# Later attention units in half-height tiles of the matrix array, and a new written order

## The chip, the cores and the metric

The kernel runs on one core of one Trainium2 chip. The metric is the device time of one execution, in microseconds, as the median of several runs. Inside a core, TensorE multiplies matrices, VectorE (DVE), ScalarE (ACT) and GpSimd (POOL) do elementwise work, and SyncE (SP) issues DMAs. Each engine runs its own list of instructions in order and waits for the others through semaphores.

## The reference

Windowed attention over 4 batches, 8 heads, 576 positions and head size 64, followed by two gated feed-forward layers over the 2304 tokens. Heads 0 to 3 are "plain" (a window of 32 neighbours), heads 4 to 7 "dilated" (32 positions, every fourth one).

```python
scores = scale * np.matmul(q, k.transpose(0, 1, 3, 2))
mask_plain = (rel >= 0) & (rel < window)
mask_dil = (rel >= 0) & (rel < window * dilation) & (rel % dilation == 0)
scores = np.where(masks[None, :, :, :], scores, -1000000000.0)
attn = np.exp(scores - np.max(scores, axis=-1, keepdims=True))
attn = attn / (np.sum(attn, axis=-1, keepdims=True) + 1e-09)
x = np.matmul(attn, v)                      # tokens x 512
h = x @ w_in; x = (h - np.tanh(h)) @ w_out  # d_ff 2048
return ((x @ w1) * (x @ w2) @ w3) @ wo      # d_ff 1024
```

## The kernel before

The dilated heads are reordered on the host so that their window too is 32 neighbours. Attention is cut into 12 units: a batch times one third of the positions (three query tiles of 64). Each unit has two parts, `p` (plain heads) and `d` (dilated heads), and each part two pairs of heads; a pair's two heads lie one above the other in the 128 partitions of `q` and `k`. `q` is stored with zeros beside each head (lines 1149 to 1152, host code), so that a product over all 128 rows gives the scores of one head alone.

The scores of a part (`at_scores`, L480 to L512) begin with one bf16 product that writes the mask into PSUM (L496), and add 24 float32 products (L508): 32 queries by 64 keys each, on a tile of the array of 128 rows and 32 columns, four of which lie side by side. The compiler makes two TensorE instructions of each float32 product, so a unit has 96. The scores of the part's two pairs are interleaved in the free dimension (`k e`). VectorE takes the maximum and subtracts it (L526, L529), ScalarE the exponential (L535), VectorE sums and inverts (L541 to L546), GpSimd multiplies (L551). TensorE turns the result (`at_T`, L561, three transposes a part), ScalarE copies it out of PSUM twice, each time with a zero on every other row (`at_Tcopy`, L574), and TensorE multiplies it by `v` (`at_pv`, L592): 12 float32 products a part, 24 instructions, on tiles of 128 rows and 64 columns, two of which lie side by side, with 64 moving columns. ScalarE and VectorE split the result into two float32r summands in `X` (L614, L619).

The feed-forward layer runs in steps: `h` (L635, 12 float32r products of 128x128 weights), tanh, subtraction, split, `y` (L725, 12 products). The first feed-forward group (3 column blocks of d_ff) is woven into the attention by hand: the string `ORDER` lists words, and the program is written out in that order. A word is a letter, a number and, for parts, `p` or `d`: `q`, `v` load, `s` scores, `M` maximum, `E` exponential, `N` sum and inverse, `m` multiply, `T` transposes, `C` copies, `P` products with v, `X`, `L` the two summands; `w` loads a weight (512 KB), `a`, `b`, `c` rebuild its float32 value from float64 bits (ScalarE L144; VectorE L149 and L153; VectorE L159 and L162), `i`, `o` split it; `h`, `t`, `g`, `G`, `k`, `y`, `Y`, `Z` are the parts of a feed-forward step; `K` prepares masks. `q`, `v` and `w` all go through SP's one queue, in the order of the words. Units 0 to 2 have homes of their own for `q` and `v` (inside `Y` and `vhomes`), and their parts go one by one; from unit 3 on (`n >= PB`) scores, maximum, exponential and sum of both parts go together. Weights are staged in two buffers, so `w2` waits for `c0`, `w3` for `c1`. PSUM is tight: one tile of two banks for scores, one bank for transposes, two for `x`; two buffers `pb` (`NPB`) hold copied transposes.

The first dense product `h0` needs `L0p L1p L2p` (all positions of the plain heads) and `L0d L1d`. After the written order come the other feed-forward groups, then the second layer, which are dense products to the end.

Of the kernel before, what the change touches and what calls it, by code (L numbers as in the profile page):

```python
# [8 lines left out]
F32 = mybir.dt.float32  # L9
# [26 lines left out]
R = 4  # L36
# [17 lines left out]
i3 X2d M4 t1 a4 m3p T3p k0 o2 L2d q5p E4 q5d g1 o3 y0 w5 h2 v3p q6p G1 s5 C3p v3d b4 c4 t2 k1 m3d  # L54
T3d g2 q6d i4 o4 a5 N4 C3d h3 m4p M5 t3 E5 b5 P3p c5 v4p T4p v4d C4p y1 N5 X3p L3p g3 P3d G2 X3d m4d
T4d i5 k2 C4d L3d s6 M6 q7p q7d o5 P4p v5p X4p L4p h4 t4 m5p y2 Y2 G3 E6 P4d X4d w6 g4 h5 T5p Z2 C5p
m5d s7 N6 G4 L4d v5d P5p k3 y3 t5 g5 a6 X5p G5 T5d C5d w7 k4 a7 b6 k5 v6p m6p L5p y4 h6 M7 q8p t6
T6p c6 g6 q8d y5 q9p C6p i6 h7 G6 v6d E7 b7 t7 c7 g7 P5d N7 k6 w8 G7 Y5 m6d s8 q9d X5d P6p X6p Z5
T6d k7 h8 v7p m7p y6 L5d C6d P6d t8 M8 a8 E8 g8 G8 q10p m7d h9 N8 m8p X6d v7d T7p C7p s9 T7d o6 k8
t9 g9 y7 C7d h10 M9 t10 L6p g10 T8p G9 v8p E9 i7 N9 b8 P7p L6d X7p w9 y8 h11 k9 m8d L7p Y8 q10d s10  # L60
q11p G10 t11 C8p m9p P7d g11 q11d Z8 X7d P8p X8p L7d L8p T8d k10 y9 G11 M10 h12 c8 y10 E10 k11 C8d
t12 v8d m9d v9p a9 v9d y11 w10 T9p C9p g12 h13 G12 P8d b9 Y11 k12 Z11 t13 N10 m10p g13 T9d m10d G13
s11 M11 P9p X8d L8d C9d X9p k13 c9 E11 y12 w11 T10p h14 y13 C10p T10d t14 g14 a10 b10 G14 P9d k14
N11 m11p L9p C10d v10p h15 t15 v10d y14 g15 G15 Y14 h16 v11p T11p t16 k15 Z14 g16 y15 X9d o7 L9d G16
k16 m11d P10p X10p h17 C11p c10 t17 v11d P10d g17 G17 y16 L10p X10d T11d C11d h18 a11 t18 P11p X11p
L10d L11p P11d k17 X11d w12 g18 y17 L11d Y17 b11 Q0 i8 G18 i9 c11 h19 Z17 k18 t19 o8 g19 h20 G19 h21
w13 t20 y18 k19 i10 y19 h22 g20 t21 g21 G20 G21 k20 i11 k21 y20 a12 h23 b12 o9 a13 b13 t22 g22 G22
o10 o11 Z20 k22 Y20 h24 c12 t23 c13 g23 i12 y21 G23 y22 o12 k23 i13 y23 t24 g24 G24 o13 k24 Z23 Y23
"""


# [9 lines left out]
def attn_moe_kernel(  # L81
# [358 lines left out]
    def window(t, half):  # L440

        return 32 * half if t else 0

    def load_v(n, parts=AB):
        if n < NU:
            b, g = units[n]
            for ty in parts:
                v = v_home(n).rearrange("p (h t c) -> p h t c", h=2, t=TU)
                for e in range(2):

                    for t0, t1 in ((0, 1), (1, TU)) if g == 0 else ((0, TU),):
                        src = vt[b, 2 * ty + e, :HW, TU * g + t0:TU * g + t1].rearrange("k t c -> k (t c)")
                        ap = [list(d) for d in src.ap]
                        step = ap[0][0] * window(TU * g + t0, 1)
                        nc.sync.dma_start(
                            out=v[e:128:2, :, t0:t1].rearrange("k h t c -> k h (t c)"),
                            in_=bass.AP(tensor=src.tensor, offset=src.offset, ap=[ap[0], [step, 2], ap[1]]),
                        )
                vs[n, ty] = v

    NB = 2 * TU

# [4 lines left out]

    def bank_of(n, ty):

        if n >= PB:  # L470
            return ust[n]["both"][:, ty]
        m = order0.index((n, ty))
        if 2 <= m < 4:

            return yA.tile([128, 2, 256], F32, tag=f"y{m - 2}", name=f"s{m}").rearrange("p a c -> p (a c)")
        if m % 4 == 0:
            banks0["s"] = attn_pools["psS"].tile([128, 2, 512], F32, tag="s", name="s")
        return banks0["s"][:, m % 2]

    def at_scores(n, parts=AB):  # L480
        b, g = units[n]
        if n not in ust:
            ms = attn_pools["sm"].tile([128, 2, 2, NB], F32, tag="ms", name="ms")
            if n == 2:
                pm = Yf[:, KC * NT - 6 * KW - 2 * NB * HW:KC * NT - 6 * KW]
                pm = pm.rearrange("p (u i k e) -> p u i k e", u=2, i=TU, e=2)
            else:
                pm = attn_pools["pp"].tile([128, 2, TU, HW, 2], F32, tag="pm", name="pm")
# [3 lines left out]
        ps = ust[n]["ps"]  # L492
        for ty in parts:
# [20 lines left out]
    def of_parts(n, parts):  # L514

        s = ust[n]
        if len(parts) == 2:
            both = s["both"][:, :, :NB * HW].rearrange("p u (i k e) -> p u i k e", i=TU, e=2)
            return [(both, s["mx"], s["pm"], [128, 2, TU, HW, 2])]
        return [(s["ps"][u], s["mx"][:, u], s["pm"][:, u], [128, TU, HW, 2]) for u in parts]  # L520

    def at_max(n, parts=AB):
        for ps, mx, pm, shape in of_parts(n, parts):
            both = len(shape) == 5
            mx = mx.rearrange("p u (i e) -> p u i e" if both else "p (i e) -> p i e", e=2)
            nc.vector.tensor_reduce(  # L526
                out=mx, in_=ps.rearrange("p u i k e -> p u i e k" if both else "p i k e -> p i e k"), axis=AX.X, op=ALU.max
            )
            nc.vector.tensor_tensor(  # L529
                out=pm, in0=ps, in1=mx.unsqueeze(len(shape) - 2).to_broadcast(shape), op=ALU.subtract  # L530
            )

    def at_exp(n, parts=AB):
# [2 lines left out]

    def at_norm(n, parts=AB):
        s = ust[n]
        pm, sm = (s["pm"], s["sm"]) if len(parts) == 2 else (s["pm"][:, parts[0]], s["sm"][:, parts[0]])
        both = len(parts) == 2  # L540
        nc.vector.tensor_reduce(  # L541
            out=sm.rearrange("p u (i e) -> p (u i) e" if both else "p (i e) -> p i e", e=2),
            in_=pm.rearrange("p u i k e -> p (u i) e k" if both else "p i k e -> p i e k"), axis=AX.X, op=ALU.add
        )
        nc.vector.tensor_scalar(out=sm, in0=sm, scalar1=1e-9, scalar2=None, op0=ALU.add)
        nc.vector.reciprocal(out=sm, in_=sm)  # L546

    def at_mult(n, parts=AB):
        s = ust[n]
        for u in parts:  # L550
            nc.gpsimd.tensor_tensor(  # L551
                out=s["pm"][:, u], in0=s["pm"][:, u],
                in1=s["sm"][:, u].rearrange("p (i e) -> p i e", e=2).unsqueeze(2).to_broadcast([128, TU, HW, 2]),
                op=ALU.mult,
            )

    def at_T(n, parts=AB):
        for u in parts:
            pt = attn_pools["psT"].tile([128, TU, 128], F32, tag="t", name="t")
            for i in range(TU):  # L560
                nc.tensor.transpose(  # L561
                    pt[:, i], ust[n]["pm"][:, u, i].rearrange("p k e -> p (k e)"), id_sb
                )
            ust[n]["pt"][u] = pt

    npb = [0]
# [1 line left out]
    def at_Tcopy(n, parts=AB):  # L568
        for u in parts:
            pt = ust[n]["pt"][u]  # L570
            pb = ust[n]["pt"][u] = attn_pools["pb"][:, npb[0] % NPB]
            npb[0] += 1
            for e in range(2):
                nc.scalar.activation(  # L574
                    out=pb[:, :, :, e], in_=pt.rearrange("p i (j q) -> p i j q", j=4), func=ACTF.Copy,
                    scale=sel_sb[:, e:e + 1],
                )

    def at_pv(n, parts=AB):
        s = ust[n]  # L580
        for ty in parts:
            x = attn_pools["psX"].tile([128, 2, TU * QT], F32, tag="x", name="x")
            v = vs.pop((n, ty))
            for i in range(TU):
                for half, h in ((0, 0), (0, 1), (1, 0), (1, 1)):
                    dst = x[64 * h:64 * h + 64]
                    if ty:
                        dst = dst[:, :, QT * i + HQ * half:QT * i + HQ * half + HQ]
                    else:

                        dst = dst.rearrange("p e (r c l) -> p c e l r", r=R, l=HQ // R)[:, 2 * i + half]
                    nc.tensor.matmul(  # L592
                        out=dst, lhsT=v[:, half, i, D * h:D * h + D],
                        rhs=s["pt"][ty][:, i, 2 * h + half].rearrange("p a q -> p (a q)"), start=True, stop=True,
                    )
            s["x"][ty] = x

    def places(n, ty):

# [578 lines left out]
```

## Time and profile before

| | us |
|---|---|
| median of 3 runs | 800.28 (800.1 to 801.37) |
| the profiled execution, its own time | 802.01 |
| its span, first to last instruction | 800.2 |
| TensorE busy in it | 779.9 |
| VectorE busy | 548.1 |
| ScalarE busy | 292.8 |
| GpSimd busy | 158.3 |

The span leaves out 1.8 us of the profiled execution at its two ends. The page gives totals, forty slices, the DMA queues, the chain of work that ended last and the costliest lines; the timeline, the windows and the groups by line answer narrower questions.

### The profile page before, as it was taken

What the parts mean: (1) busy time and instruction counts of PE and PEld (TensorE: products, weight loads), DVE (VectorE), ACT (ScalarE), POOL (GpSimd) and SP (SyncE); (2) the same over time, 40 slices, a digit from 0 to 9 for tenths busy, and PEclk for the clock granted to TensorE, in tenths of its full rate; (3) what the DMA queues carried; (4) which work ended last, traced back from release to release, by engine and by line L of the source; (5) the groups of instructions that cost most, each with busy time, mean ns of one, the idle gap of its engine ahead of it and who ended that gap; (6) DMA issues with size and microseconds to landing.
All of it is one profiled execution on the core that took longest, in us unless ns stands there. A gap on an engine that the chain in (4) does not pass through costs nothing.

```text
span 800.2 us, 14174 instructions
## 1 busy us (share of the span) xinstructions
PE 779.9 (97%) x5592; PEld 688.0 (86%) x5592; DVE 548.1 (68%) x909; ACT 292.8 (37%) x546; POOL 158.3 (20%) x153
## 2 busy tenths in 40 slices
PE   5699999999999999999999999999999999999998
PEld 4589999888889888898888898799998999899996
DVE  4998675668888779987888889954454544734431
ACT  3566565443444444444444444321122111311111
POOL 3363343500022001210022223211121111211111
PEclk9799999999999999999999999999999999999999
DMA  9988742114455253632554344296203750156302
GB/s 300 302 247 294 236 155 73 53 53 126 150 160 158 105 162 116 186 119 66 156 155 136 105 134 131 93 340 211 93 1 115 238 187 1 41 181 202 118 1 79
DMA packets 62018, 115.58 MB, mean 144 GB/s; under 512 B 6400, under 2 KB 27008, under 8 KB 61952
## 3 DMA queue, kind: packets, MB, share of 16 engines
q1 hardware_dynamic: 61664, 114.32, 44.8%
q8 instruction: 44, 0.72, 0.4%
q10 hardware_dynamic: 288, 0.36, 0.2%
q14 instruction: 22, 0.18, 0.1%
HBM read 95.26 MB, written 19.40 MB: 143 GB/s over the span
## 4 chain that ended last, share of the span: by engine, by line
PE 89%; DVE 8%; ACT 1%; DMA 1%; issue 1%; ACTq 0%; SPq 0%; DVEq 0%
PE h L635 26%; PE y L725 25%; PE pr L979 22%; PE o L1042 6%; PE pr L1042 6%; PE x L592 2%; DVE a L159 2%; PE s L508 2%; DVE a L162 1%; DVE a L153 1%; PE t L561 1%; DVE a L149 1%; DVE Y L872 1%; DVE ms L541 1%; DMA id_sb<-in_ident 0%
## 5 line engine op out<-in xcount | busy, mean ns | idle before, releaser
L725 PE MATMUL y<-gs,LT 128*128 128x512 f32 (+1 forms) x520 | 121.9, 368 | 0.0
L725 PEld LDWEIGHTS y<-gs,LT 128*128 128x128 f32 x520 | 92.1, 188 | 16.3
L635 PE MATMUL h<-X,LT 128*128 128x512 f32 (+1 forms) x471 | 104.9, 370 | 0.0
L635 PEld LDWEIGHTS h<-X,LT 128*128 128x128 f32 x471 | 82.8, 188 | 15.2
L683 DVE TENSOR_TENSOR th<-h,th 128x512 f32<-128x512 f32 (+1 forms) x83 | 51.3, 618 | 58.5 <-ACT th L677 58.3
L979 PE MATMUL pr<-X 128*128 128x384 f32 x435 | 81.8, 334 | 0.0
L979 PE MATMUL pr<-X,LT 128*128 128x384 f32 x405 | 80.7, 336 | 0.0
L635 PE MATMUL h<-X,w 128*128 128x512 f32 (+1 forms) x381 | 78.8, 352 | 0.0
L677 ACT ACTIVATE th<-h 128x512 f32<-128x512 f32 (+1 forms) x83 | 44.8, 540 | 87.4 <-PE h L635 87.4
L979 PEld LDWEIGHTS pr<-X 128*128 128x128 f32 x435 | 76.2, 188 | 0.5
L159 DVE SCALAR_TENSOR_TENSOR a<-st,a 128x512 uint32<-128x512 uint32 x68 | 75.2, 1107 | 0.3
L979 PEld LDWEIGHTS pr<-X,LT 128*128 128x128 f32 x405 | 71.9, 188 | 1.3
L635 PEld LDWEIGHTS h<-X,w 128*128 128x128 f32 x381 | 62.8, 188 | 10.6 <-DVE th L683 0.2
L690 ACT ACTIVATE gs<-th 128x512 fp32r<-128x512 f32 (+1 forms) x83 | 47.9, 577 | 64.5 <-DVE th L683 57.5
L1016 DVE TENSOR_TENSOR u<-pr,u 128x384 f32<-128x384 f32 x72 | 40.1, 557 | 45.1 <-PE pr L979 38.5
L725 PE MATMUL y<-gs,w 128*128 128x256 f32 (+1 forms) x352 | 70.4, 330 | 0.0
L144 ACT ACTIVATE a<-st 128x512 f32<-128x512 f32 x68 | 45.5, 670 | 59.7 <-DMA st<-in_w 21.0
L992 ACT ACTIVATE cs<-u 128x384 fp32r<-128x384 f32 x24 | 12.6, 526 | 149.4 <-DVE u L1016 149.4
L1034 POOL TENSOR_TENSOR Y<-w,v 128x384 f32<-128x384 f32 x24 | 24.5, 1019 | 212.8 <-DVE w L1016 212.8
L725 PEld LDWEIGHTS y<-gs,w 128*128 128x128 f32 x352 | 54.6, 188 | 6.5
L162 DVE SCALAR_TENSOR_TENSOR a<-st,a 128x512 uint32<-128x512 uint32 x68 | 54.8, 806 | 2.3
L170 POOL TENSOR_TENSOR LT<-a,LT 128x512 fp32r<-128x512 f32 x18 | 25.8, 1436 | 152.2 <-ACT LT L167 152.2
(169 smaller groups left out, 1259.5 us busy)
## 6 DMA issues: line engine op xcount, KB each, us to landing
st<-in_w SPq DMA_DIRECT2D x28, 512.0 KB, 3.5
LT<-p SPq DMA_DIRECT2D x56, 256.0 KB, 4.2
X<-p SPq DMA_DIRECT2D x56, 256.0 KB, 4.7
st<-in_w_in SPq DMA_DIRECT2D x16, 512.0 KB, 4.2
st<-in_w_out SPq DMA_DIRECT2D x16, 512.0 KB, 4.1
q<-in_qz SPq DMA_DIRECT2D x18, 384.0 KB, 5.3
p<-LT SPq DMA_DIRECT2D x26, 256.0 KB, 4.5
v<-in_vt SPq DMA_DIRECT2D x32, 192.0 KB, 4.6
```

The costliest lines, as they stand in the source:

```text
L144: nc.scalar.activation(out=a.bitcast(F32), in_=st[:, :, 1].bitcast(F32), func=ACTF.Abs)
L159: nc.vector.scalar_tensor_tensor(out=a, in0=st[:, :, 1], scalar=0xC0000000, in1=a, op0=ALU.bitwise_and, op1=ALU.bitwise_or)
L162: nc.vector.scalar_tensor_tensor(out=a, in0=st[:, :, 0], scalar=29, in1=a, op0=ALU.logical_shift_right, op1=ALU.bitwise_or)
L170: nc.gpsimd.tensor_tensor(out=lo, in0=a.bitcast(F32), in1=hi.bitcast(F32), op=ALU.subtract)
L635: nc.tensor.matmul(out=ps, lhsT=a[sel[0]], rhs=b[sel[1]], start=(start and i == 0), stop=(i == n - 1), **kw)
L677: nc.scalar.activation(out=th[:, :tn], in_=gst[i][:, :tn], func=ACTF.Tanh)
L683: nc.vector.tensor_tensor(out=th[:, :tn], in0=ps[:, :tn], in1=th[:, :tn], op=ALU.subtract)
L690: nc.scalar.activation(out=gs[:, 0, :tn], in_=th[:, :tn], func=ACTF.Copy)
L725: nc.tensor.matmul(out=y[k], lhsT=wt[sel[0]][:, 128 * k:128 * k + 128], rhs=gs[:, sel[1], tn * m:tn * m + tn], start=(cs[m] == 0 and n == ...
L979: nc.tensor.matmul(out=ps[:, :TP], lhsT=s[e][:, 128 * k:128 * k + 128], rhs=(hi, lo)[f][1][k], start=start and n == 0, stop=n == 5, skip_g ...
L1016: nc.vector.tensor_tensor(out=out, in0=ps[:, :TP], in1=x, op=op)
L1042: nc.tensor.matmul(out=tiles[m], lhsT=cs[e][:, 128 * m:128 * m + 128], rhs=WW[j][f], start=begin and n == 0, stop=end and n == 2,)
```

## The change

The change concerns units 3 to 11 and the written order; the arithmetic is the same.

Scores (`scores_by_rows`): each product now takes only the 64 rows of its own head, on a tile of 64 rows and 32 columns. The two heads of a pair lie on the two row halves and write to the two banks of the unit's PSUM tile; the two pairs of heads lie on different columns. There are as many products as before, 48 a unit, 96 instructions, now on eight tiles. Two mask products a unit, as before.

Everything after the scores is laid out with the 64 keys of one head next to each other, plain and dilated side by side, so that a transpose puts the plain keys of a head on one row half and the dilated on the other. One copy a part then suffices, without zeros. The products with v (`at_pv`) take 64 rows, 64 columns and 32 moving columns, on four tiles: 48 products a unit, 96 instructions, where there were 24 and 48. They now come once a unit, `P3` instead of `P3p` and `P3d`, and need both transposes' copies (both `pb` buffers) and both `x` banks at once. `v` is loaded so that one buffer holds one pair of each kind, each kind on 64 neighbouring partitions, in the same number of DMAs and bytes.

For units 0 to 2 only the PSUM banks of the scores change: every third score tile takes a bank of the `s` tile, the others `y0` and `y1`.

The words are the same but for `P`; they stand in a new order throughout. Up to `h0`:

```diff
-K0 K1 q0p q1p s0p q2p q0d M0p q1d s1p E0p s2p s0d M1p N0p m0p w0 T0p E1p C0p N1p M2p q2d M0d E2p m1p
-N2p T1p v0p s1d v1p m2p s2d w1 a0 E0d C1p T2p b0 P0p C2p N0d c0 M1d X0p M2d E1d v2p a1 m0d L0p b1
-T0d q3p E2d P1p C0d w2 a2 q3d P2p N1d c1 m1d T1d s3 N2d C1d i0 m2d i1 T2d b2 c2 v0d v1d X1p L1p w3
-P0d o0 X2p L2p o1 X0d i2 M3 P1d L0d X1d E3 a3 L1d q4p q4d h0 v2d s4 N3 C2d P2d w4 b3 t0 g0 h1 G0 c3
...
+w0 q0p q1p w1 q2p q0d a0 b0 K0 K1 c0 s0p s1p s2p q1d q2d a1 w2 M0p v0p E0p M1p i0 b1 c1 s0d M2p N0p
+E1p E2p m0p i1 M0d v1p s1d E0d N1p m1p a2 T0p M1d C0p N2p E1d m2p s2d q3p q3d v2p T1p P0p C1p T2p
+C2p N0d M2d X0p w3 m0d b2 P1p N1d q4p m1d s3 o0 o1 X1p c2 L0p L1p T0d C0d v0d a3 T1d P2p E2d X2p P0d
+q4d v1d M3 E3 s4 v2d b3 c3 i2 L2p C1d N2d N3 X0d m2d w4 P1d L0d X1d q5p m3p T2d C2d L1d a4 h0 M4 t0
+g0 P2d q5d T3p b4 E4 o2 w5 i3 N4 G0 m3d h1 s5 C3p o3 t1 k0 T3d g1 v3p v3d h2 m4p a5 X2d C3d q6p q6d
...
```

After `h0` the products with v stand in 17 separate blocks on TensorE before (a neighbouring pair of parts twice) and in 10 after; `s4` stands behind `h0` before and ahead of it after. The rest of the diff, cut to its core:

```diff
     def bank_of(n, ty):
-        if n >= PB:
-            return ust[n]["both"][:, ty]
         m = order0.index((n, ty))
-        if 2 <= m < 4:
...
-        if m % 4 == 0:
+        if m % 3:
+            y = yA.tile([128, 2, 256], F32, tag=f"y{m % 3 - 1}", name=f"s{m}")
...
+    def scores_by_rows(n, g):
...
+        for i in range(TU):
+            t = TU * g + i
+            for ty in AB:
+                k, q = kq[ty]
+                for h in range(2):
+                    r = slice(64 * h, 64 * h + 64)
+                    for e in range(2):
+                        for half in range(2):
+                            k0 = KS[t] - KS[TU * g] + window(t, half)
+                            j, c = 2 * e + half, QT * h + HQ * half
+                            nc.tensor.matmul(
+                                out=ps[HQ * j:HQ * j + HQ, h, i, 1 - ty], lhsT=q[r, e, i, c:c + HQ],
+                                rhs=k[r, e, k0:k0 + HW], start=False, stop=(i == TU - 1 and ty == 1),
+                                skip_group_check=True, tile_position=(64 * h, HQ * j),
+                            )
...
     def at_Tcopy(n, parts=AB):
...
+            if n >= PB:
+                pb = ust[n]["pt"][u] = pb.rearrange("p i j e q -> p (i j e q)")[:, :TU * 128]
+                nc.scalar.activation(out=pb, in_=pt.rearrange("p i c -> p (i c)"), func=ACTF.Copy)
+                continue
             for e in range(2):
                 nc.scalar.activation(
...
     def at_pv(n, parts=AB):
...
+        for i in range(TU):
+            for half in range(2):
+                for e in range(2 if n >= PB else 0):
+                    for ty in AB:
+                        r = slice(HW * (1 - ty), HW * (1 - ty) + HW)
+                        for h in range(2):
+                            c = 128 * i + QT * e + HQ * half
+                            nc.tensor.matmul(
+                                out=x_part(n, ty, i, half, h)[:, e], lhsT=v[e][r, half, i, D * h:D * h + D],
+                                rhs=s["pt"][h][r, c:c + HQ], start=True, stop=True,
+                                tile_position=(r.start, 64 * h),
+                            )
...
```

## Rows read from the trace of the kernel before

**Rows 1.** Page, parts 1 and 2: engine totals; GB/s over 40 slices of 20 us

```profile
PE 779.9 (97%) x5592; PEld 688.0 (86%) x5592; DVE 548.1 (68%) x909; ACT 292.8 (37%) x546; POOL 158.3 (20%) x153
...
GB/s 300 302 247 294 236 155 73 53 53 126 150 160 158 105 162 116 186 119 66 156 155 136 105 134 131 93 340 211 93 1 115 238 187 1 41 181 202 118 1 79
```

**Rows 2.** Windows: length, busy us of PE, PEld, DVE, ACT, POOL, clock, DMA share, GB/s

```profile
0.00:36.85 36.85, 21.29 (x530) 16.60 (x530) 26.26 (x52) 15.11 (x30) 12.23 (x24) 0.89 0.93 297
36.85:130.00 93.15, 92.74 (x1731) 86.02 (x1730) 69.33 (x124) 58.34 (x128) 38.25 (x42) 0.99 0.70 222
...
32.00:36.00 4.00, 1.90 (x36) 1.90 (x38) 3.90 (x5) 0.31 (x1) 1.03 (x1) 0.50 1.00 320
```

**Rows 3.** Timeline, TensorE to 40 us: start, length, count, idle before and releaser

```profile
5.75 0.48 PE L496 MATMUL s<-mask_sb,id_sb 128*128 128x384 bf16 x1 [5.75 <-DVE mask_sb L375]
...
34.10 2.83 PE L592 MATMUL x<-pb,v 128*64 128x64 f32 x48 [2.55 <-DVE X L619]
...
36.85 2.83 PE L635 MATMUL h<-X,WG 128*128 128x256 f32 x12
```

**Rows 4.** Timeline, TensorE: one unit's mask and scores at full clock

```profile
64.27 0.49 PE L496 MATMUL s<-mask_sb,id_sb 128*128 128x384 bf16 x2
64.69 1.55 PE L508 MATMUL s<-k,q 128*32 128x64 f32 x96
66.16 0.92 PE L592 MATMUL x<-pb,v 128*64 128x64 f32 x24
```

**Rows 5.** Timeline, TensorE: blocks with v between dense blocks

```profile
121.35 0.92 PE L592 MATMUL x<-pb,v 128*64 128x64 f32 x24
122.20 1.68 PE L635 MATMUL h<-X,w 128*128 128x256 f32 x12
123.81 0.92 PE L592 MATMUL x<-pb,v 128*64 128x64 f32 x24
...
128.02 1.62 PE L592 MATMUL x<-pb,v 128*64 128x64 f32 x48
129.57 1.68 PE L725 MATMUL y<-gs,w 128*128 128x256 f32 x12
131.09 1.59 PE L635 MATMUL h<-X,WG 128*128 128x256 f32 x12
132.52 1.52 PE L635 MATMUL h<-X,w 128*128 128x256 f32 x12
```

**Rows 6.** Lines L508, L592: weight loads of 32 and 64 columns, min/median/max ns

```profile
L508 PEld LDWEIGHTS s<-k,q x864: 106/110/177, 28.4 to 108.2; 128*32 128x32 f32 x173
...
L592 PEld LDWEIGHTS x<-pb,v x576: 132/138/227, 19.7 to 129.4; 128*64 128x64 f32 x192
```

**Rows 7.** DMA issues: KB each, median us to landing

```profile
st<-in_w_in SPq DMA_DIRECT2D x16, 512.0 KB, 4.2
...
q<-in_qz SPq DMA_DIRECT2D x18, 384.0 KB, 5.3
...
v<-in_vt SPq DMA_DIRECT2D x32, 192.0 KB, 4.6
...
k<-in_kT SPq DMA_DIRECT2D x12, 224.0 KB, 5.0
```

**Rows 8.** Lines by shape, VectorE, first 38.1 us (last row whole span)

```profile
L162 DVE SCALAR_TENSOR_TENSOR a<-st,a 128x512 uint32<-128x512 uint32 x3 | 4.0, 1345 | 0.1
L526 DVE TENSOR_REDUCE ms<-s 128x6 f32<-128x384 f32 x6 | 3.3, 546 | 4.3 <-PE s L508 4.3
L159 DVE SCALAR_TENSOR_TENSOR a<-st,a 128x512 uint32<-128x512 uint32 x3 | 2.9, 983 | 0.0
...
L153 DVE TENSOR_SCALAR a<-a 128x512 uint32<-128x512 uint32 x3 | 2.3, 766 | 0.1
...
L149 DVE TENSOR_SCALAR a<-a 128x512 f32<-128x512 f32 x3 | 1.2, 396 | 0.0
...
L541 DVE TENSOR_REDUCE ms<-pm 128x12 f32<-128x768 f32 x9 | 8.5, 950 | 1.9 <-ACT pm L535 1.9
```

More of the change, by code (lines that the diff above doesn't have):

```diff
@@ L55 @@
[L55 to L59, printed above, removed]
@@ L444, in load_v @@
     def load_v(n, parts=AB):
[L445 to L459, printed above, removed]
+        if n >= NU:
+            return
+        b, g = units[n]
+        for part in parts:
+            v = v_home(n).rearrange("p (h t c) -> p h t c", h=2, t=TU)
+            for other in range(2):
+                if n < PB:
+                    rows, ty, e = slice(other, 128, 2), part, other
+                else:
+                    rows, ty, e = slice(HW * other, HW * other + HW), 1 - other, part
+                for t0, t1 in ((0, 1), (1, TU)) if g == 0 else ((0, TU),):
+                    src = vt[b, 2 * ty + e, :HW, TU * g + t0:TU * g + t1].rearrange("k t c -> k (t c)")
+                    ap = [list(d) for d in src.ap]
+                    step = ap[0][0] * window(TU * g + t0, 1)
+                    nc.sync.dma_start(
+                        out=v[rows, :, t0:t1].rearrange("k h t c -> k h (t c)"),
+                        in_=bass.AP(tensor=src.tensor, offset=src.offset, ap=[ap[0], [step, 2], ap[1]]),
+                    )
+            vs[n, part] = v
     NB = 2 * TU
@@ L492, in at_scores @@
         ps = ust[n]["ps"]
+        if n >= PB:
+            scores_by_rows(n, g)
+            return
         for ty in parts:
@@ L512, in at_scores @@
                         )
-    def of_parts(n, parts):
-        s = ust[n]
[L517 to L527, printed above, removed]
-            )
+    def scores_by_rows(n, g):
+        ps = ust[n]["both"][:, :, :NB * HW].rearrange("p h (i u k) -> p h i u k", i=TU, u=2)
+        m0 = mask_sb[:, M_DIL[g]:M_DIL[g] + TU]
+        ap = [list(d) for d in m0.ap]
+        ap.insert(2, [ap[1][0] * (M_PLAIN[g] - M_DIL[g]), 2])
+        for h in range(2):
+            nc.tensor.matmul(
+                out=ps[:, h], lhsT=id16_sb, rhs=bass.AP(tensor=m0.tensor, offset=m0.offset, ap=ap),
+                start=True, stop=False, skip_group_check=True,
+            )
+        kq = [ks.pop((n, ty)) for ty in AB]
+        for i in range(TU):
[12 more added lines that the diff above has]
+                                skip_group_check=True, tile_position=(64 * h, HQ * j),
+                            )
@@ new lines, in at_max @@
+    def at_max(n, parts=AB):
+        s = ust[n]
+        if n >= PB:
+            ps = s["both"][:, :, :NB * HW].rearrange("p h (b k) -> p h b k", k=HW)
+            pm = s["pm"].rearrange("p h (b k) -> p h b k", k=HW)
+            nc.vector.tensor_reduce(out=s["mx"], in_=ps, axis=AX.X, op=ALU.max)
+            nc.vector.tensor_tensor(
+                out=pm, in0=ps, in1=s["mx"].unsqueeze(3).to_broadcast([128, 2, NB, HW]), op=ALU.subtract
+            )
+            return
+        for u in parts:
+            ps, pm = s["ps"][u], s["pm"][:, u].rearrange("p (i k e) -> p i k e", i=TU, e=2)
+            mx = s["mx"][:, u].rearrange("p (i e) -> p i e", e=2)
+            nc.vector.tensor_reduce(out=mx, in_=ps.rearrange("p i k e -> p i e k"), axis=AX.X, op=ALU.max)
@@ L529, in at_max @@
             nc.vector.tensor_tensor(
-                out=pm, in0=ps, in1=mx.unsqueeze(len(shape) - 2).to_broadcast(shape), op=ALU.subtract
+                out=pm, in0=ps, in1=mx.unsqueeze(2).to_broadcast([128, TU, HW, 2]), op=ALU.subtract
             )
@@ L538, in at_norm @@
         s = ust[n]
[L539 to L546, printed above, removed]
+        for sm, pm in ([(s["sm"], s["pm"])] if n >= PB else [(s["sm"][:, u], s["pm"][:, u]) for u in parts]):
+            if n >= PB:
+                out, src = sm, pm.rearrange("p h (b k) -> p h b k", k=HW)
+            else:
+                out = sm.rearrange("p (i e) -> p i e", e=2)
+                src = pm.rearrange("p (i k e) -> p i e k", i=TU, e=2)
+            nc.vector.tensor_reduce(out=out, in_=src, axis=AX.X, op=ALU.add)
+            nc.vector.tensor_scalar(out=sm, in0=sm, scalar1=1e-9, scalar2=None, op0=ALU.add)
+            nc.vector.reciprocal(out=sm, in_=sm)
     def at_mult(n, parts=AB):
@@ L581, in at_pv @@
         for ty in parts:
[L582 to L591, printed above, removed]
+            s["x"][ty] = attn_pools["psX"].tile([128, 2, TU * QT], F32, tag="x", name="x")
+        v = {part: vs.pop((n, part)) for part in parts}
+        for i in range(TU):
[3 more added lines that the diff above has]
+                        r = slice(HW * (1 - ty), HW * (1 - ty) + HW)
+                        for h in range(2):
+                            c = 128 * i + QT * e + HQ * half
+                            nc.tensor.matmul(
+                                out=x_part(n, ty, i, half, h)[:, e], lhsT=v[e][r, half, i, D * h:D * h + D],
+                                rhs=s["pt"][h][r, c:c + HQ], start=True, stop=True,
+                                tile_position=(r.start, 64 * h),
+                            )
+                for h in range(2 if n < PB else 0):
+                    ty = parts[0]
                     nc.tensor.matmul(
-                        out=dst, lhsT=v[:, half, i, D * h:D * h + D],
+                        out=x_part(n, ty, i, half, h), lhsT=v[ty][:, half, i, D * h:D * h + D],
                         rhs=s["pt"][ty][:, i, 2 * h + half].rearrange("p a q -> p (a q)"), start=True, stop=True,
                     )
-            s["x"][ty] = x
     def places(n, ty):
```

56 lines of the change are left out of this document (34 added, 22 removed).

## The prediction

> **What bounds the kernel.** I read the page's totals first, then windows by stage, then TensorE's timeline. TensorE is busy 779.9 of 800.2 us [rows 1]. The windows split that: up to 36.85 us, where the first dense product `h0` begins, it is busy 21.29 us and idle 15.56; from there to 130 us, the end of attention, it is busy 92.74 of 93.15 [rows 2]. Beyond 130 us only dense products follow, which the change leaves alone. So from `h0` on, time is TensorE's work, and a microsecond taken off TensorE there is a microsecond off the end, as long as the others keep up: VectorE is busy 69.33 of these 93.15 us, ScalarE 58.34, the DMAs 0.70 [rows 2]. Ahead of `h0` TensorE isn't the limit. It waits for VectorE at 5.75 us and again at 34.10 [rows 3], VectorE is busy 26.26 of 36.85 us, and the DMAs are busy 0.93 of the time at 297 GB/s [rows 2]; the slices show hardly more than that anywhere in attention (300, 302, 247, 294) [rows 1]. The end is therefore: the time at which `h0` starts, plus TensorE's work from there (800.20 - 36.85 = 763.35 us now), plus new idle time.
>
> **Scores.** A unit's 96 score instructions take 1.47 us of TensorE, from 64.69 to the next block at 66.16 [rows 4], 15.3 ns each on four tiles side by side. An instruction with v has the same 64 moving columns, with two tiles side by side: 24 more of them in one block cost 1.55 - 0.85 = 0.70 us [rows 5], 29 ns each. So twice as many tiles halve the price, and per tile both come to about 60 ns. [...] Eight tiles then give about 7.5 ns each. What doesn't shrink is the change of tile shape at both ends of a block: a block of 24 with v takes 0.85 us, of which 0.70 is its 24 instructions, so 0.15 is fixed [rows 5]. A unit saves (1.47 - 0.15) / 2 = 0.66 us. No row shows row halves; the bounds are 0 (they take turns) and 0.66, and I take 0.66, because the columns do run side by side. The two heads write to different banks, so the banks give no reason against. Seven units (5 to 11) stand behind `h0` in both orders: -4.6 us. `s3` stands ahead of it in both. `s4` moves ahead of it, and its slot with its masks, here as in unit 6 64.27 to 66.16, goes: -1.9 us.
>
> **Products with v.** There are 96 instructions a unit for 48, on four tiles for two: per tile as many as now. Each has half the moving columns but loads the same 64 weight columns. Loads of 32 columns show 110 ns, of 64 columns 138 [rows 6], which is 0.88 ns a column, so 64 columns are about 56 ns (an estimate from this difference), as long as today's whole interval of 58 ns per tile; 32 moving columns would be half of that. The load sets the pace, and I take no change of the stream, 1.40 us a unit. The bounds: the interval halves with the moving columns (-0.70 a unit, -6.3 for nine units), or the row halves take turns (+1.40, +12.6). What does go is blocks: 17 behind `h0` become 10. One block in place of two saves 2 x 0.85 - 1.55 = 0.15 us inside, and a dense block between two of them takes 1.61 us where one away from them takes 1.43 [rows 5], so about 0.2 more; I take 0.35 x 7 = -2.5 us, with bounds of 1.0 and 3.1.
>
> [...]
>
> **Start.** The queue of loads decides first. `P1d`, the last product ahead of `h0`, needs `v1d`. Ahead of it and with it the new order sends four weights (512 KB each), ten parts of `q` (384 KB and about 215 KB of `k` each; five units, where four units' parts stood before), five parts of `v` (two DMAs of 192 KB each) and the masks [rows 7]: about 10.4 MB, where the old order sends 8.7. At 297 GB/s, start included, that is 35 us against 29. Then come `P1d` (1.4 us at half clock, from the 2.75 us for two parts), its copy, and `h0`: 37.5 us at the earliest. VectorE is the second limit. `b3`, `c3` and `N3` now stand ahead of `L1d`: 0.4 + 0.8 + 1.0 + 1.3 us and about 1.5 us (0.95 of it the sum) [rows 8], 5 us more. Part of them finds room: `b0` and `c0` go to the front, into the 5.75 us in which all waited for masks and the 4.3 us in which VectorE waited for scores [rows 3, 8]. But `b0` stands ahead of `K0` on VectorE and needs `w0`, which shares the first microseconds with the masks, so the first mask product comes at some 8 us in place of 5.75; what hides that is the loads, which couldn't feed scores faster anyway. In sum `L1d` moves from about 38 to 39.5 us. I put `h0` at 39.0 (37.5 to 42), +2.15 us. `h0` begins at a low clock now, 0.50 in the stretch ahead of it, after idle time on TensorE [rows 2], and its 12 products take 2.83 us where they take some 1.6 later [rows 3, 5]; the new order idles there as well, and I count it as equal.
>
> **Behind h0.** The new layout gives ScalarE one copy a part for two, about 10 us less in all, on an engine that isn't the limit; VectorE and GpSimd do the same operations on neighbouring instead of interleaved elements, counted at nothing since neither is full. The new waits: `P` of a unit needs both copies and both `x` banks, so it waits for the last `L` of the unit before, and `h`, `y`, `T` behind it in TensorE's queue wait too; the next unit's first copy waits for `P` to free a `pb` buffer, and tanh and the splits queue behind that copy on ScalarE. Between two `P` some four dense blocks (6 us) lie, enough for chains of 2 to 3 us. Loads are closer: `q5`, needed by `s5` three blocks behind `h0`, ends at about 12 MB, 41 to 44 us, just when `s5` is due. New idle time: +1.0 us (0 to 4).
>
> **Sum.** Work from `h0` on: 763.35 - 4.6 - 1.9 - 2.5 = 754.35. With `h0` at 39.0 and 1.0 idle, the span is 794.35, 5.85 less. Against the profiled execution (802.01, span 800.2 and 1.8 around it) that is 796.2; the median of the runs shown is 800.28, 1.7 below it, so the forecast is 794.4.
>
> **Rivals.** (1) Row halves take turns on TensorE. Scores save nothing (+4.6 behind `h0`), and products with v cost double, 1.40 x 9 = +12.6: 811.6 us. It decides the sign once more than about a third of that price comes true (5.9 of 17.2). For it speaks that no tile of fewer than 128 rows is in this trace; against it that tiles divided by columns do run together. (2) Issue is the floor: 15.3 ns is what an instruction costs at least. Scores save nothing (+4.6), v costs 96 x 15.3 = 1.47 for 1.40 (+0.6): 799.6, no change. [...] (3) Weight loads of 64 rows aren't the pace, and v halves: 794.4 - 6.3 = 788.1. [...] (4) The start or the loads limit: `h0` at 42 and 4 us of idle time give 800.4.
>
> **Chances.** Forecast 0.64 (790 to 798.5), v halves 0.10, loads limit 0.10, issue floor 0.07, turns 0.09. A difference under 0.2%, 1.6 us, can't be told from none here: same is 798.7 to 801.9. Faster: 0.64 + 0.10 + 0.01 of the floor + 0.03 of the loads = 0.78; same 0.10; slower 0.12. The range 787 to 801 holds the forecast, v halved, the floor and most of the loads' case, and leaves out the turns.
>
> **What would show it.** A unit's scores should take 0.81 us from start to the next block, its products with v 1.5 us in one block of 96; `h0` should begin near 39 us with `s4` behind it already, and TensorE should show under 2 us of idle time to the end of attention, which should come near 124 us. Scores at 1.47 with v at 1.5 would be the floor; v near 3 us the turns; v near 0.85 the third rival; idle time ahead of `s5` or the early `P` the loads. I would be wrong most easily in the start, which rests on a count of bytes.

## The result, and the profile after

The changed kernel takes 807.45 us (median of 4 runs, 807.13 to 809.77), the kernel before 800.39 beside it: a ratio of 1.0092, 95% interval [1.0072, 1.0113]. It is slower, by 7 us or 0.9%, where 794.4 was forecast, and the range (787 to 801) doesn't hold it. The profiled execution took 807.13 us, of which 805.30 are the span.

The page first (parts 1 and 3): TensorE runs 432 more product instructions than before, and as many more weight loads, and is busy 3.4 us less [rows 1]; the queue `q8` of kind "instruction" carries 47 packets.

```profile
span 805.3 us, 15000 instructions
...
PE 776.5 (96%) x6024; PEld 684.9 (85%) x6024; DVE 541.6 (67%) x909; ACT 282.5 (35%) x528; POOL 156.3 (19%) x153
...
q8 instruction: 47, 0.77, 0.4%
```

Windows by stage (length, busy us of PE, PEld, DVE, ACT, POOL, clock, DMA share, GB/s): to `h0`, from there to the first dense product of 512 columns, which is the end of attention's work, and the rest.

```profile
0.00:39.89 39.89, 22.07 (x628) 16.65 (x629) 26.20 (x59) 17.20 (x33) 15.39 (x27) 0.89 0.96 306
39.89:138.94 99.05, 92.38 (x2098) 86.65 (x2097) 64.15 (x117) 47.36 (x113) 36.27 (x41) 0.98 0.69 192
138.94:805.30 666.36, 662.07 (x3302) 581.55 (x3300) 451.29 (x734) 217.93 (x384) 104.60 (x85) 1.00 0.40 127
```

Before, the same two marks stand at 36.85 and 133.88 us ([rows 2] ends the stretch at 130 us):

```profile
36.85:133.88 97.03, 96.62 (x1764) 89.90 (x1763) 73.11 (x131) 60.92 (x134) 39.99 (x44) 0.99 0.67 213
133.88:800.20 666.32, 662.01 (x3302) 581.53 (x3300) 448.78 (x728) 216.75 (x382) 106.07 (x86) 1.00 0.40 126
```

The rest hasn't moved. `h0` came at 39.9, near the forecast (39.0). The loss is in the middle: with 4.6, 1.9 and 2.5 us off and 1.0 of new idle time it should have been 89.0, and it is 99.05, of which TensorE is idle 6.67 (0.41 before). This is what those idle times wait for:

```profile
PE x L638 <- issue: 4.2, 3, 2.4
PE s L542 <- DMA q<-in_qz: 1.3, 1, 1.3
PE h L687 <- issue: 0.7, 1, 0.7
PE x L638 <- DMA v<-in_vt: 0.5, 2, 0.3
```

"issue" means that the profile shows no semaphore that held the instruction back: 4.9 of the 6.67 us have no releaser. Such an idle time is called a pause here. The timeline of TensorE (start, length, count, idle before) shows the blocks at their good and at their bad:

```profile
67.02 1.17 PE L542 MATMUL s<-k,q 64*32 64x64 f32 x96
68.12 1.70 PE L777 MATMUL y<-gs,WG 128*128 128x256 f32 x12
69.75 1.36 PE L638 MATMUL x<-pb,v 64*64 64x32 f32 x78
71.40 0.53 PE L638 MATMUL x<-pb,v 64*64 64x32 f32 x18 [0.29 <-issue]
...
78.63 1.59 PE L638 MATMUL x<-pb,v 64*64 64x32 f32 x95
82.57 0.21 PE L638 MATMUL x<-pb,v 64*64 64x32 f32 x1 [2.35 <-issue]
82.71 0.90 PE L598 MATMUL t<-id_sb,pm 128*128 128x128 f32 x3
83.27 2.62 PE L777 MATMUL y<-gs,w 128*128 128x256 f32 x12
85.73 1.57 PE L687 MATMUL h<-X,w 128*128 128x256 f32 x12
...
93.42 1.60 PE L638 MATMUL x<-pb,v 64*64 64x32 f32 x96
94.95 0.55 PE L598 MATMUL t<-id_sb,pm 128*128 128x128 f32 x3
```

A unit's scores take 1.10 us here to the next block, and 1.17 on average over the seven units behind `h0`, waits left out (forecast 0.81, 1.47 before [rows 4]); its products with v take 1.53 (93.42 to 94.95; forecast 1.5). At 78.63 one block stops after 95 of its 96 products for 2.35 us, with nothing to wait for. Behind this pause TensorE also runs at a lower clock: the `y` block at 83.27 takes 2.46 us to the next one, where 1.45 is usual, in a window whose granted clock is 0.55. The shorter pauses at 60.57 and 70.89 us have no such window behind them: from 60 to 78 us the granted clock is 1.00.

```profile
78.63:82.57 3.94, 1.59 (x96) 1.49 (x96) 0.98 (x2) 1.23 (x2) 0.00 (x0) 0.93 0.94 322
82.57:85.73 3.16, 3.16 (x16) 3.02 (x16) 0.00 (x0) 1.28 (x4) 0.00 (x0) 0.55 1.10 252
```

**Where the pauses sit.** I counted TensorE's list (products, weight loads and its own semaphore instructions, in order) and looked up the pauses, and the packets of `q8` beside them. One of 0.34 us at 23.20 us (place 662) is left out, since run 3 puts the same wait down to GpSimd (`POOL pm`):

```
place in list   mod 256   TensorE stands (start to start)   q8 packet        end to restart
  449             193       16.25 to 17.70                   15.02 - 16.11    1.59
 1217             193       35.97 to 37.50                   35.24 - 36.20    1.30
 2241             193       60.57 to 62.30                   59.69 - 60.74    1.56
 2753             193       70.89 to 71.40                   68.52 - 69.86    1.54
 3265             193       80.00 to 82.57                   80.11 - 81.03    1.54
 4801             193      114.81 to 115.81                 112.93 - 114.27   1.54
```

All six stand at the same place of a block of 256, and TensorE goes on 1.3 to 1.6 us after a packet of 16 KB has landed. 47 packets, at 256 entries each, would be 12,032, and the list has some 12,180 entries. Before it had 11,330, by 44 packets, and no idle time of 0.05 us or more at such a place. The page of before has:

```profile
q8 instruction: 44, 0.72, 0.4%
```

So the reading to be tested: the list reaches TensorE in blocks of 256, each by one packet, and these blocks come too late. A unit has 96 entries more than before. (The expectations below count 542 and 446 a unit; from the masks of `s3` to the dense part, over nine units, it is some 533 now and 439 with the old products in the same order.) The packet of 80.11 us shared the DMA engines with loads that kept them busy; this is the DMA view from 78.63 to 82.57 us:

```profile
DMA packets 977, 1.27 MB, mean 322 GB/s; under 512 B 59, under 2 KB 896, under 8 KB 976
...
q1 hardware_dynamic: 976, 1.25, 92.7%
q8 instruction: 1, 0.02, 1.5%
...
v<-in_vt SPq DMA_DIRECT2D x4, 192.0 KB, 8.8
```

### The profile page after: what moved, and what is told of

Its sections match the earlier page's. It is cut to its first block, busy times and chain, and to the rows that moved or that the text cites. A ratio compares the mean times of both kernels' runs of the same rounds, so it can differ in the third digit from the quotient of the medians.

```text
span 805.3 us, 15000 instructions
## 1 busy us (share of the span) xinstructions
PE 776.5 (96%) x6024; PEld 684.9 (85%) x6024; DVE 541.6 (67%) x909; ACT 282.5 (35%) x528; POOL 156.3 (19%) x153
## 4 chain that ended last, share of the span: by engine, by line
PE 88%; DMA 4%; DVE 4%; SPq 2%; issue 1%; ACT 1%; ACTq 0%
PE h L687 26%; PE y L777 24%; PE pr L1031 22%; PE o L1094 6%; PE pr L1094 6%; DMA v<-in_vt 2%; PE x L638 2%; PE s L542 1%; DMA st<-in_w_out 1%; DVE a L159 1%; DMA st<-in_w_in 1%; PE t L598 1%; DVE a L162 1%; SPq L460 1%; DVE Y L924 1%
## 5 line engine op out<-in xcount | busy, mean ns | idle before, releaser
L159 DVE SCALAR_TENSOR_TENSOR a<-st,a 128x512 uint32<-128x512 uint32 x68 | 73.7, 1083 | 0.4
L162 DVE SCALAR_TENSOR_TENSOR a<-st,a 128x512 uint32<-128x512 uint32 x68 | 51.6, 759 | 2.3
```

Of the source, the lines that this page charges most:

```text
L159: nc.vector.scalar_tensor_tensor(out=a, in0=st[:, :, 1], scalar=0xC0000000, in1=a, op0=ALU.bitwise_and, op1=ALU.bitwise_or)
L162: nc.vector.scalar_tensor_tensor(out=a, in0=st[:, :, 0], scalar=29, in1=a, op0=ALU.logical_shift_right, op1=ALU.bitwise_or)
```

## The experiments

The expectations set a theory of late instructions against rivals: first, that the new order costs the time; later, that the length of the list costs it whatever the data do. "Stretch" is `h0` to the first 512-column product, "dense part" what follows it.

**1 and 2: the two halves of the change alone.** The first has the old tiles and products in the new order and the joined blocks; the second the new tiles in the old order, the joined block where the later of the two stood.

```
e1: -P3            e2: -P3p ... P3d       (units 3 to 11)
    +P3p P3d           +        P3
```

> Old products (128 rows) and old layout, written in the new order (each P as both parts in turn). Theory A, late instructions: TensorE's gaps without a releaser in the changed kernel (7.3 us to 120 us, each at an instruction whose place in TensorE's list is 193 more than a multiple of 256) come from a denser instruction stream; with 446 instead of 542 instructions a unit they go, scores cost 0.33 us a unit more (9 units, +3): about 802 us. Theory B, the order itself is the loss: the gaps and the late start stay and the scores cost more: 809 to 811 us.

Measured: 798.68 us against 800.56, ratio 0.9981 [0.9970, 0.9992]. The stretch:

```profile
37.30:129.67 92.37, 92.20 (x1667) 86.60 (x1666) 64.42 (x117) 57.95 (x131) 36.47 (x42) 1.00 0.67 210
```

Idle 0.16 us, and 97.03 - 92.37 = 4.66 us less than before; the prediction's terms for `s4` and the blocks were 1.9 + 2.5 = 4.4. The order costs nothing. It is a small gain, 1.9 us by the medians and 4.1 by the spans of the two traces (796.1 for 800.2): the stretches here and below are those of one execution each, and run 1's ten executions lie between 797.5 and 800.7 us. Theory A had the time 3 us too high, but the pauses at place 193 are gone as it said, except one of 1.59 us at place 1217, ahead of `h0`. So what makes the change slow comes with the new tiles and their layout.

> New products and layout, written in the old order; only the products with v of a unit are joined (put where the last of their inputs is ready, the plain part's X and L behind them, h12 and t12 behind L8p), and four half-size buffers for copied transposes stand in the place of two. Theory A: the gaps without a releaser stay (5 to 8 us), against 3 us won by scores and 3 by joined blocks: 801 to 804 us. Theory B: the old order gives 794 to 796 us, as the prediction's sum has it without the start.

Measured: 828.07 us, ratio 1.0343. Neither theory gave this: in the old order a joined block waits for the splits of the unit before and for its own `v`, which two blocks a stage apart did not. The waits of TensorE from 35 to 161 us:

```profile
PE x L640 <- DVE X L673: 6.0, 2, 4.2
PE x L640 <- DMA v<-in_vt: 5.9, 2, 3.7
PE x L640 <- issue: 2.3, 2, 1.5
```

The run says that the new order is needed for joined blocks, and nothing of the instructions.

**3: the same kernel, its list moved by 128 entries.** 64 products of 64 columns on the zero tile are put ahead of everything.

```
-ORDER = "w0 q0p ..."
+ORDER = "S64 w0 q0p ..."
```

> The changed kernel with 64 small products (128 instructions) that nothing uses at the head of TensorE's list, where it waits for masks. Theory A: the gaps stay at places that are 193 more than a multiple of 256 and so fall on other products, 128 instructions earlier in the program; their sum changes (4 to 9 us) and the time with it, 803 to 810 us. Theory C, the products or their tiles themselves stall: the gaps stay at the same products and the time within 1 us of 807.5.

Measured: 807.53 us, ratio 1.0089. That the time is that of the changed kernel is chance: in the trace `h0` comes at 36.13 us, the stretch takes 101.61 with 10.13 idle, and the dense part 1.7 us more. The pauses: places 705, 961, 1217, 1473, 1985, 2241, 2753, 3265 and 4289, every one 193 above a multiple of 256. The instructions that stand at these places are now others: from `h0` on, two `h` blocks (3.0 us idle) and a block with v of an early unit, in old tiles (2.0 us), which had no pause there, and three blocks with v in new tiles (3.8 us). Two of these three paused in the changed kernel too, after 78 and after 95 of their 96 products. Here it is after 14 and after 31, earlier by just the 64 products that were put ahead:

```profile
68.71 0.43 PE L638 MATMUL x<-pb,v 64*64 64x32 f32 x14
70.25 1.47 PE L638 MATMUL x<-pb,v 64*64 64x32 f32 x82 [1.11 <-issue]
...
78.37 0.66 PE L638 MATMUL x<-pb,v 64*64 64x32 f32 x31
80.56 1.14 PE L638 MATMUL x<-pb,v 64*64 64x32 f32 x65 [1.53 <-issue]
```

So it is the place in the list and not what the instruction does.

**4: less data.** From the fourth unit on the 64-row tiles read only half of each `q` tile; the other half are zeros which the old tiles needed. Loading without them saves 3.5 MB and leaves the list as it is.

```
-q = home(n, 2 * TU * 2 * QT, ...); out=q, in_=qz[...]
+q = home(n, 2 * TU * QT, ...);     out=q, in_=qc[...]      # n >= PB
```

> The changed kernel, but from unit 3 on q is loaded without its zeros, which 64-row products don't need: 192 KB in place of 384 for each of 18 parts, 3.5 MB less in all. Theory A, with transfers of instructions waiting behind transfers of data: gaps without a releaser shrink by 2 to 4 us, the waits for q (1.7 us) go: 802 to 805 us. If the gaps had nothing to do with transfers: only the waits for q go, 805 to 806.5 us.

Measured: 799.55 us, ratio 0.9987 [0.9977, 0.9997]: 8 us come back with the same list, more than either theory gave. `h0` 36.87, and the stretch:

```profile
36.87:130.26 93.39, 90.70 (x2099) 84.75 (x2098) 64.06 (x117) 47.58 (x113) 37.04 (x42) 1.00 0.65 178
...
PE s L544 <- issue: 1.2, 1, 1.2
PE x L640 <- issue: 1.0, 3, 0.5
PE h L689 <- issue: 0.3, 1, 0.3
```

Idle is 2.69 for 6.67 us, and the granted clock of the stretch is 1.00 (0.98 in the changed kernel). Between the two traces 3.0 us are the earlier `h0` and 5.7 the stretch. There the pauses fall from 4.9 to 2.5 us and the waits for `q` and `v` from 1.8 to 0.2, so not all that came back is the list's.

**5 to 8: which part of the change needs the entries.** 5 keeps the row scores and takes the products with v back to 128 rows, from copies that have the other type's rows zeroed (as many entries a unit as before); 6 is 5 with the `q` of run 4; 8 is the reverse of 5, row products with v and old scores; 7 has the old products and 24 more of one column a unit, as many entries as the changed kernel.

```
e5: -rhs=pt[h][r, c:c+HQ], tile_position=(r.start, 64*h)      (96 a unit)
    +rhs=pt[h][:, :, c:c+HQ]                                  (48, pt zeroed by type in the copy)
e8: -lhsT=q[r, ...], rhs=k[r, ...], tile_position=(64*h, HQ*j)
    +lhsT=q[:, ...], rhs=k[:, ...], tile_position=(0, HQ*j)
e7: +nc.tensor.matmul(out=ps[...][:, i, :1, e], lhsT=q[:, e, i, ...], rhs=zero_sb)   (on e1)
```

> Scores in 64-row tiles and the new layout and order, but products with v over all 128 rows again: two zeroed copies a part, 24 products (48 instructions) a unit for 96, x held by pair of heads and split by two instructions a part on ScalarE and VectorE. 446 instructions a unit as before. Theory A (late instructions): the gaps without a releaser all but go, as with the old products in this order (798.7 us), and scores at 1.15 us for 1.48 win 3 us on that: 795 to 797 us. If row halves were the loss: 800 us or more.

> The same with q loaded without its zeros from unit 3 on. Theory A: fewer bytes ahead of h0 and no late instructions: 793 to 796 us, below every kernel so far. If the half q helped the changed kernel only by easing late instructions: as the kernel without it, within 1 us.

> Old products in the new order, with 24 products more a unit: one moving column of zeros added to a score, so 96 instructions more a unit (542), with almost no work in them (some 7 to 11 ns each pair, 3 to 5 us in all). Theory A: density of instructions alone brings gaps of 3 to 8 us at places 193 more than a multiple of 256: 805 to 811 us. If the gaps come from the tiles or the layout: none, 802 to 804 us.

> The changed kernel with its scores over all 128 rows on four tiles again (the zeros of q do the rest), products with v in 64-row tiles. 542 instructions a unit. Theory A: gaps of 4 to 8 us stay, scores cost 0.33 us a unit more: 807 to 811 us. If 64-row scores were the loss and products with v harmless: 799 to 801 us.

Measured:

```
      time     ratio to before          h0     stretch  idle   dense part
e5    803.61   1.0039 [1.0024,1.0054]   39.07   93.03   1.46   669.72
e6    801.68   1.0012 [1.0001,1.0022]   37.97   91.82   1.03   670.16
e7    809.73   1.0114 [1.0096,1.0133]   39.37   98.04   1.89   669.71
e8    805.91   1.0076 [1.0048,1.0103]   39.98   97.52   2.74   666.40
```

By its time alone 5 would speak for the rival (800 us or more), but its stretch is 6 us shorter than the changed kernel's, and what it lacks is in the dense part. 8 carries most of the loss: a block of 96 products with v takes 1.53 us and one of 48 takes 1.55 (e1), so the 96 more entries a unit buy nothing and bring pauses, at places 1985, 2241, 3265 and 4801. With the row scores alone the stretch is 93.03. Added up over the stretch, the pauses at place 193 of 256 are 4.9 and 8.7 us in the changed kernel and run 3, 2.7 in 8 and 1.8 in 7, which have the long list, and 0 before and in 1, 0.5 in 5 and 0 in 6, which have the short one. In 7 the longer list costs 4.4 us of stretch against run 12 below (98.04 - 93.63), but only 1.5 of it is more idle time; the rest is the products' own time (a unit's scores take about 2.0 us for 1.48). So a longer list alone gives fewer pauses than the theory wanted of it; that entries which themselves take time also give the blocks time is my reading. And in 5, 6 and 7 the dense part, whose instructions are the same in all kernels, takes 3.3 to 3.8 us more. None of the theories had that, and it is by luck that 7 lies in the range of theory A (805 to 811 us).

**9 to 12: the dense part.** 5 and 6 add a tile of 8 bytes a partition, 7 one of 4, ahead of the large tiles, and so move their addresses. 9, 10 and 11 are 5, 6 and 7 with 64 bytes in its place; 12 is run 1 with an 8-byte tile that nothing reads.

```
e9, e10: -rows_sb = const.tile([128, 2], F32)
         +rows_sb = const.tile([128, 16], F32)[:, :2]
e12:     +gap_sb = const.tile([128, 2], F32)       # on e1; one memset, no reader
```

> The kernel of e5_row_scores_only (64-row scores, products with v on all 128 rows from zeroed copies, joined; the list is as long as before) whose added constant tile takes 64 bytes of each partition instead of 8, so that all that lies behind it in SBUF is moved by 64 bytes instead of 8. In e5 the dense part after the last attention product took 669.7 us against 666.4 in the kernel before, with the same instructions. If the moved addresses are the cause: that part back to 666.4 +-0.5, and the time 800.3 (799.6 to 801.2). If they are not: 803.6 as e5. The attention stretch stays at 93 us by both.

> e6_row_scores_half_q (as e5, and q without its zeros from the fourth unit on: 3.5 MB less to load) with the same 64-byte tile. By the late-instruction theory with the addresses mended: the attention stretch 91.8 as in e6, the dense part 666.4, the time 798.2 (797.4 to 799.2). If the late dense part comes from the order or from the products: 801.7 as e6.

> e7_more_instructions (the old products in the new order, and 24 products of one column a unit more, so that the list is as long as the changed kernel's) with its added tile taking 64 bytes instead of 4. If the addresses made the dense part 3.3 longer there: that part 666.4 and the time 806.4 (805.5 to 807.3). What is over e1's 798.7 is then the cost of 96 more instructions a unit alone, waits for the list and their own time together: 7.7. If not the addresses: 809.7 as e7.

> e1_old_tiles_new_order with an 8-byte tile that nothing reads put where e5 has its added one: the same instructions but one memset, all later SBUF addresses moved as in e5. If the addresses cost the dense part its 3.3 us: that part 669.7 and the time 802.0 (801.2 to 802.8), against e1's 798.7. If they do not: 798.7 (798 to 799.5).

Measured:

```
      time     ratio to before          h0     stretch  idle   dense part
e9    804.64   1.0053 [1.0038,1.0068]   37.48   95.80   4.04   668.83
e10   800.79   1.0003 [0.9992,1.0015]   38.57   92.03   1.06   669.25
e11   808.26   1.0102 [1.0085,1.0119]   38.77   98.47   2.43   668.80
e12   802.81   1.0023 [1.0014,1.0032]   38.48   93.63   0.41   669.61
```

Moving by 64 bytes takes off 0.9 us of it in each of the three and doesn't mend it; but run 12 shows that an unused tile is enough: 4.1 us more than run 1, 3.2 of them in the dense part. This is not idle time: products themselves take longer, though not all. Set beside run 1 one by one, over half of the 3,300 start as far behind the one before as there, to a nanosecond; most others take up to 20 ns more, some less, and 2.8 of the 3.2 us lie in the first half. (9 also missed its stretch, 95.80 for 93: of its 4.04 us idle 2.2 wait for `q` and `v` and 1.0 for the list.) Lines by shape in the dense part (busy us, mean ns), of run 12:

```profile
L726 PE MATMUL y<-gs,LT 128*128 128x512 f32 x416 | 106.7, 391 | 0.0
L636 PE MATMUL h<-X,LT 128*128 128x512 f32 x383 | 94.0, 391 | 0.0
L636 PE MATMUL h<-X,w 128*128 128x512 f32 x245 | 61.5, 395 | 0.0
```

and of run 1:

```profile
L725 PE MATMUL y<-gs,LT 128*128 128x512 f32 x416 | 106.1, 389 | 0.0
L635 PE MATMUL h<-X,LT 128*128 128x512 f32 x383 | 93.6, 390 | 0.0
L635 PE MATMUL h<-X,w 128*128 128x512 f32 x245 | 60.5, 392 | 0.0
```

**13 and 14: nothing moved, and still less data.** 13 is 6 with its two columns in the last bytes of the warm-up tile. 14 is 4 with one unit's `k` used for all later units, 3.2 MB less to load at the same list.

```
e13: -rows_sb = const.tile([128, 2], F32)
     +rows_sb = warm[:, 508:512].bitcast(F32)
e14: +if n > PB + 1: k = kept[ty]        # no tile and no load
```

> e6_row_scores_half_q (64-row scores, joined products with v on all 128 rows, q without its zeros from the fourth unit on) whose two marker columns lie in the last 8 bytes of the warm-up tile, so that no address is moved. By what e12 showed (an 8-byte tile that nothing uses makes the dense part 3.2 us longer): dense part 666.4, attention stretch 91.8 as in e6, time 798.2 (797.3 to 799.2), level with e1's 798.7 or just under it. If instead the products or the copies make the dense part longer: 801.7 as e6.

> e4_half_q (the changed kernel with q loaded without its zeros) which from the sixth unit on doesn't load its k and computes with the fifth unit's instead: 3.2 MB less to load, and a wrong output by that. TensorE's list is the same. If the waits at fixed places of the list come from the list's blocks being held up by the data's transfers: e4's idle of 2.7 us in the attention stretch falls below 1.3, the stretch from 93.4 to 91.5 to 92.3, the time from 799.55 to 798 (797 to 798.8). If the blocks are late whatever the data do: idle 2.7 as in e4 and 799.5.

13: 799.20 us against 801.10, ratio 0.9979 [0.9970, 0.9987]; dense part 666.84. The addresses were what held 5 and 6 back.

```profile
38.41:130.56 92.15, 90.63 (x1666) 84.83 (x1665) 68.80 (x135) 60.00 (x150) 36.46 (x41) 0.99 0.62 175
130.56:797.40 666.84, 662.09 (x3302) 581.61 (x3300) 450.77 (x734) 217.45 (x384) 103.85 (x85) 1.00 0.40 127
```

It is no better than run 1 (0.9981): the row scores take 7.80 us for 10.35 in the stretch (8.57 with the waits inside them), and the 2.5 that they save go to `h0`, 1.1 us later, and to 1.4 us more idle time. 1 and 13 can't be told apart; of the kernels that leave no work out they have the lowest ratios, with 4 hardly behind.

14: 798.42 us, ratio 0.9968 [0.9955, 0.9981]. Idle went from 2.69 to 1.40 us, near the 1.3 expected, and the pauses in it from 2.5 to 0.9, so they do follow the data. The stretch didn't follow: 93.70 for 93.39, where 91.5 to 92.3 was expected. The time is in the expected range, but its interval overlaps that of 4, so the times alone don't tell the two apart. One pause over 0.2 us was left in the stretch, and this is what came behind it:

```profile
75.42 2.93 PE L785 MATMUL y<-gs,w 128*128 128x256 f32 x12 [0.77 <-issue]
78.15 1.90 PE L695 MATMUL h<-X,w 128*128 128x256 f32 x12
```

2.73 us to the next block and 1.73 behind it, where 1.45 and 1.5 are usual: 1.5 us on top of the 0.77 of the pause, and so all that the shorter idle time (1.29) had brought. In the window from 75 to 90 us the granted clock was 0.89, in those on either side 1.00.

## Why the prediction was wrong

The span came out at 805.30 for 794.35, 10.95 us more. By the prediction's own terms:

- **New idle time, +1.0 (0 to 4), was 6.26 (6.67 less the 0.41 of before): +5.3.** This is the step that failed. The prediction looked for idle time in the chains between engines and in the loads; the loads did bring some (1.8 us for `q` and `v`). It asked what 96 more instructions a unit cost on TensorE and never how they get there. 4.9 us of the idle time are waits for the list itself. That these hang on the place in the list is shown by run 3, that it takes the longer list by runs 1 and 5 (0 and 0.5 us with the short one), and that they shrink with the data by runs 4 and 14 (4.9, 2.5 and 0.9 us with 0, 3.5 and 6.7 MB less to load). How a packet comes to be held up behind data isn't seen in a trace. The page of before had a row for it (part 3: 44 packets, 0.72 MB, of kind "instruction"), which isn't among the rows that I read.
- **Scores, -0.66 a unit, were -0.30: +2.5 over seven units** (7 x 1.17, their mean without the wait for `q`, for 7 x 0.81). The mechanism was right and the size was not. In the block at 67.02 the first 32 products start 8.4 ns apart on average, mostly 6 to 7, near the forecast 7.5; the other 64 start 10.2 ns apart. Each of the 96 is two entries of the list, a weight load and a product, so that the whole block runs at 5.7 ns an entry. Whether the issue of entries is the limit there no run settles; the steps of 6 to 7 ns, two entries each, speak against a fixed 5.7 ns an entry.
- **Around the pauses, 0 was taken, and about +2.3 is left over.** Set beside run 1, idle time left out, the blocks with v take 1.1 us more (15.87 for 14.79), above all those that a wait cuts in two, and the `h` and `y` blocks 1.2 more, of which the one at the lower clock, at 83.27 us, is 1.0.
- **`h0`: +0.9** (39.89 for 39.0), inside its bounds, but partly by luck: two of the pauses, 1.2 us each, stand ahead of it (up to 17.70 and 37.50 us), and run 1, in the same order with one, has it at 37.30. The 2.75 us in the prediction's sum for the start are the 48 instructions at 34.10 us, to the next block at 36.85 [rows 3].
- **From span to median: +2.1.** The forecast took the profiled execution as 1.7 us slower than the median. The profile after is 0.3 faster than its median. A single execution isn't worth such a correction.

What came true: products with v at 1.53 us a unit. A weight load of 64 columns takes 135 ns for 64 rows and 138 for 128 (medians, both in the changed kernel):

```profile
L638 PEld LDWEIGHTS x<-pb,v x864: 129/135/135, 49.9 to 133.1; 64*64 64x64 f32 x173
...
L645 PEld LDWEIGHTS x<-pb,v x144: 132/138/231, 21.9 to 42.6; 128*64 128x64 f32 x144
```

That agrees with the load setting the pace, as the prediction had it. The number of entries doesn't: the scores' block has as many and takes 1.10 us. What also came true: `s4` and the joined blocks, 4.66 us in run 1 for 4.4; and the dense part, untouched. Of the rivals, the turns fell (v would have been near 3 us), v halved fell (0.85), and the issue floor of 15.3 ns fell (the scores' block runs at 11.5 a product). The loads' rival (800.4) named 4 us of idle time and had the wrong thing late: mostly not the data of a product, but the product itself.

The chances followed from this. Nearly all that was given to times over 801 hung on one mechanism, the row halves, with 0.09. That a kernel with a fifth more instructions in a stretch, ahead of which and in which the DMAs are busy 0.93 and 0.70 [rows 2], might be held up by its own instructions was no case at all. Waits for the list needn't be many: run 1 has one pause at place 193 (1.6 us idle, ahead of `h0`), the changed kernel six, 7.3 us in all.

## What to carry to other kernels

The smaller tiles of the products with v took 96 instructions a unit for 48, so price a tile's list entries beside its products: count them a microsecond in the stretch, and look at the DMA share there and at the instruction queue on the page. Where TensorE is idle with no releaser, count its place in the list; pauses that all stood at one place of 256 were late instructions here, and loading 3.5 MB less (8 us) was worth more than the faster scores (2.5 us in run 13). And when an experiment adds a tile, run one that adds the tile alone (3.2 us in the dense part of run 12), or put it where nothing moves (run 13: 666.84 us for run 6's 670.16).

## What the hardware showed that was not expected

- The packets of `q8` in the changed kernel, 47 of 16 KB, would at 256 entries each make about its list of some 12,180 entries, and a pause there ends 1.3 to 1.6 us after its packet, in six pauses of six. With the DMA engines 0.94 busy at 322 GB/s, the packet of the longest pause started only after TensorE had stopped (80.11 for 80.00).
- On eight fp32 tiles of 64 x 32, with a weight load for each product, products start mostly 6 to 7 ns apart at first and 10.2 ns on average later (the block at 67.02 us: 8.4 over the first 32, 10.2 over the other 64).
- A weight load of 64 columns takes as long for 64 rows as for 128 (135 and 138 ns), and twice as many half-row products on twice as many tiles take a unit as long: 1.53 and 1.55 us.
- Moving the large SBUF tiles by 8 bytes made the dense part 3.2 us longer in run 12 (669.61 for 666.42), moving them by 64 bytes 2.4 to 2.8 in runs 9 to 11. Why isn't known; beside these only 4 bytes were tried (run 7, 3.3).
